# Gated linear attention with a SiLU MLP: q scaled by the reciprocal of alpha's reverse product instead of by a second scan

## The chip, the cores and the metric

The kernel runs on one core of one Trainium2 chip. The metric is the device time of one execution in microseconds. Profiles show one execution, taken by the hardware profiler. The engines are named PE (TensorE, the matrix products), DVE (VectorE), ACT (ScalarE), POOL (GpSimd) and SP (SyncE, which issues most transfers).

## The reference

Two blocks follow each other. The first is a recurrent attention over 4 batches of 8 heads, 768 tokens and a head dimension of 48; the second is an MLP with SiLU on the 3072 tokens of 384 features that come out of it.

```python
for t in range(S):
    state = alpha[:, :, t, :, None] * state + np.einsum('bhd,bhe->bhde', k[:, :, t], v[:, :, t])
    y[:, :, t] = np.einsum('bhd,bhde->bhe', q[:, :, t], state)
...
h = x @ w_in
g = h * (1.0 / (1.0 + np.exp(-h)))
return (g @ w_out).astype(np.float32)
```

All of alpha lies between 0.8 and 1. The weights `w_in` (384 x 2048) and `w_out` (2048 x 384) arrive in double precision and are converted on the chip.

## The kernel before, in words

**Chunks.** Each of the 4 sequences of 768 tokens is cut into 6 chunks of 128 tokens: 24 chunks, numbered n = 0 to 23. Within a chunk the recurrence is turned into products. Let u(t) be the product of alpha over the tokens after t up to the chunk's end, and P the product over the whole chunk. Then k(t) u(t) is the key as it counts at the end of the chunk, and q(t) / u(t) is the query that takes this back to its own token. Scores are products of the two, with later tokens masked out; what earlier chunks left in the state `st` counts with the factor P. All of it is per feature, and the tiles hold the 8 heads as 4 pairs, with the features on the partitions and 4 segments of 129 places along the row: one separating place and 128 tokens. A row so has 4 x 129 = 516 places.

**What VectorE does for a chunk** (function `products`, lines 766 to 793, and `quotient`, lines 795 to 812):

- L775: a scan over the row from right to left multiplies alpha up into `u`. The constant tile `one` starts each segment anew.
- L778: the first place of each segment, the product P over the chunk, goes to `least`, held above 2^-64.
- L786, or L790 and L792: `kp` = k times `u`.
- L803: the reciprocal of the four values of `least`, put at the segment starts of the tile `inv`, which holds zeros elsewhere.
- L805: a second scan, from left to right, multiplies alpha up onto 1/P. It gives `p` = (alpha(1) ... alpha(t)) / P, which is 1/u(t).
- L812: `p` = q times `p`, the scaled query.

Both scans read the tile `al` of alpha, which ScalarE copies out of PSUM (L764) for the first chunks, and VectorE transposes into place (L739) for the later ones.

**Two stages.** For n below 8 (`NA`), `products` calls `quotient` directly, and both follow the order in which they are written, as do the instructions marked `settled`. From n = 8 on, the work of a step is spread over four slots: scores of the chunk before, `products`, `quotient`, and then values, states and `flip`. There the VectorE instructions are placed by a scheduler, which interleaves them with other work, while TensorE's products keep the order in which they are written.

**Other work on the same engines.** The MLP runs beside the attention in pieces that `fill` hands out by due times: products with `w_in` into three PSUM banks `ps_m` (first `enter_plain`, later `enter`, which combines blocks so as to need fewer products, with sums `xc` and `wx` of blocks made ahead of them), the SiLU on ScalarE, sums on VectorE (L1018, L1106, L1123), and products with `w_out` into `ps_o` (`leave`). VectorE also converts the weights in the first 110 us (L675 to L678) and, later, reduces alpha and the weights to their extremes (L728), by which a flag is set at the end. Attention ends at about 435 us; the rest is MLP.

**Buffers.** `u` has one buffer (`upool`), `kp` two in the first stage and one later, `p` two.

Of the kernel before, what the change touches and what calls it, by code (L numbers as in the profile page):

```python
# [8 lines left out]
F32 = mybir.dt.float32  # L9
# [5 lines left out]
ALU = mybir.AluOpType  # L15
# [341 lines left out]
def quotients(  # L357
# [20 lines left out]
    dve, act, gps = nc.vector, nc.scalar, nc.gpsimd  # L378
# [9 lines left out]
    def settled(ins):  # L388

        return tc.keep_in_program_order(ins) if stated[0] else ins  # L390
# [13 lines left out]
    NP = H // 2  # L404
# [6 lines left out]
    W = C + 1  # L411
# [7 lines left out]
    def pool(name, bufs=1, space=None):  # L419
        kw = {} if space is None else {"space": space}  # L420
        return ctx.enter_context(tc.tile_pool(name=name, bufs=bufs, **kw))
# [3 lines left out]
    fix = pool("fix")  # L425
# [20 lines left out]
    def ps_attn(n=C):  # L446
        return ps_a.tile([128, 512], F32, name="ps_a").rearrange("p (j c) -> p j c", c=n)
# [37 lines left out]
    def load(n, names="akq"):  # L485
        if n == NT:
            return
        c = ctxs.setdefault(n, dict(zip(("ci", "b"), divmod(n, B))))
        b, rows = c["b"], slice(c["ci"] * C, c["ci"] * C + C)
        for name, src in (("a", alpha), ("k", k), ("q", q)):  # L490
            if name not in names:
                continue
            x = src[b, :, rows, :]
            if n < NA:
                c[name] = nat[name][n % NIN]
                settled(nc.sync.dma_start(c[name][:, :, 0:D], x.transpose([1, 0, 2])))
                continue

            c[name] = late["quads"][name]
            for u in range(2):
                for i in range(2):
                    r = 64 * u + 32 * i
                    nc.sync.dma_start(
                        c[name][r : r + 32, 32 * (1 - i) :][:, 0 : 4 * NP * D].rearrange(
                            "p (g c) -> p g c", g=NP),
                        x[u::2].rearrange("h (b j) d -> b h (j d)", j=4))
# [40 lines left out]


    seg = [(fix if i == 0 else spare).tile([128, NP * W + 1], F32, name=f"al{i}") for i in range(2)]
    inv = fix.tile([128, NP * W + 1], F32, name="inv")

    kps = [(spare if i else fix).tile([128, NP, C], F32, name=f"kp{i}") for i in range(2)]
    qps = [(spare if i else fix).tile([128, NP * W + 1], F32, name=f"p{i}") for i in range(2)]
# [1 line left out]
    def turns(x, n):  # L557

        return x[(n + 1) % 2]
# [2 lines left out]
    gps.memset(seg[0], 0.0)  # L562
    gps.memset(one, 0.0)
    gps.memset(one[:, 0 : NP * W + 1 : W], 1.0)
    for t in [inv] + seg[1:]:
        gps.memset(t, 0.0)


# [11 lines left out]
    least = fix.tile([128, NT, NP], F32, name="least")  # L580
# [152 lines left out]
    def tokens(t):  # L733

        return t[:, 1 : NP * W + 1].rearrange("p (j c) -> p j c", c=W)[:, :, 0:C]

    def turned(x, to):
        x = x[:, 32:].rearrange("p (g j d) -> p g j d", j=4, d=D)
        dve.transpose(to.rearrange("p g (b j) -> p g j b", j=4), x[:, :, :, 0:32])  # L739

    def bring(n, names="akq"):

        c = ctxs[n]
        sg = seg[0 if late else n % 2]
        ps = c.setdefault("ps", {})

        for name in names:
            if n >= NA:
                if name == "a":
                    turned(c[name], tokens(sg))  # L750
                    load(n + 1, "a")
                continue
            if n <= GB and name != "a" or n == 6 and name == "q":

                at = "kq".index(name)
                ps[name] = (bank(at) if n == 1 else out_bank(at, 512)).rearrange("p (j c) -> p j c", c=C)
            else:
                ps[name] = ps_attn()
            if n == 0 and name != "a" or n == 1 and name != "q":
                idle(2)  # L760
            for j in range(NP):
                pe.transpose(ps[name][:, j, :], c[name][:, 2 * j : 2 * j + 2, :], ident)
            if name == "a":
                settled(act.copy(tokens(sg), ps[name]))  # L764

    def products(n):

        if "ps" not in ctxs[n]:
            bring(n)
        c = ctxs[n]  # L770
        sg = seg[0 if late else n % 2]
        ps = c.pop("ps")
        end = NP * W
        u = upool.tile([128, end + 1], F32, name="u")
        settled(dve.tensor_tensor_scan(u[:, end - 1 :: -1], sg[:, end:0:-1], one[:, end:0:-1],  # L775
                                       0.0, ALU.mult, ALU.add))

        settled(dve.tensor_single_scalar(least[:, n, :], u[:, 0:end:W], 2.0**-64, ALU.max))  # L778
        kp = c["kp"] = turns(kps, n) if n < NA else kps[0]
        ut = tokens(u)  # L780
        if n >= NA:
            ps["k"] = late["turn"].tile([128, NP, C], F32, name="turn")
            turned(c["k"], ps["k"])
            load(n + 1, "k")
        if n < NA:
            settled(dve.tensor_tensor(kp, ps["k"], ut, ALU.mult))  # L786
            quotient(n, sg, ps["q"])
            return
        j = NP // 2
        dve.tensor_tensor(kp[:, 0:j], ps["k"][:, 0:j], ut[:, 0:j], ALU.mult)  # L790
        k, ut = [x[:, j:].rearrange("p j (e c) -> p j e c", e=2) for x in (ps["k"], ut)]
        dve.tensor_tensor(kp[:, j:].rearrange("p j (e c) -> p j e c", e=2)[:, :, ::-1], k, ut, ALU.mult)  # L792
        c["sg"] = sg

    def quotient(n, sg=None, q=None):

        c = ctxs[n]
        if sg is None:
            if n < NA:
                return  # L800
            sg = c.pop("sg")
        end, iv = NP * W, inv
        settled(dve.reciprocal(iv[:, 0:end:W], least[:, n, :]))  # L803
        p = turns(qps if n < NA else [qps[0], late["p"]], n)
        settled(dve.tensor_tensor_scan(  # L805
            p[:, 0:end], sg[:, 0:end], iv[:, 0:end], 0.0, ALU.mult, ALU.add))
        qp = c["qp"] = tokens(p)
        if q is None:
            q = late["turn"].tile([128, NP, C], F32, name="turn")
            turned(c["q"], q)  # L810
            load(n + 1, "q")
        settled(dve.tensor_tensor(qp, q, qp, ALU.mult))  # L812
# [475 lines left out]
    def start():  # L1288

        nonlocal bridged  # L1290
        w = lambda upto: convert(0, upto)
        products(0)
        products(1)
        load(NIN)
        next(conv[0])
# [19 lines left out]
        bring(2, "kq")  # L1315
        w(6)
        products(2)
        go_on()
        w(7)
# [37 lines left out]
    for step in range(5, STEPS):  # L1357
        stages = [[(scores, 1)], [(products, 0)], [(values, 1)], [(states, 1)]]
        if step < NA:
            stages = stages[0:2] + [stages[2] + stages[3], []]  # L1360
        elif step >= NA:
            stages = [[(land, 1), (scores, 1)], [(products, 0)], [(quotient, 0)],
                      [(values, 1), (states, 1), (flip, 0)]]
        for slot, group in enumerate(stages):
            for stage, lag in group:
                n = step - lag
                if not 0 <= n < NT:
                    continue
                stage(n)
                if stage is values:  # L1370
                    bridged = n + 1
                if stage is states and n + 1 + NIN < NA:
                    load(n + 1 + NIN)
                if stage is states and n + NV < NT:
                    load_v(n + NV)
            if step * SLOTS + slot == (NA + 1) * SLOTS - 1:
                x = decayed.rearrange("p (o i c) -> p o i c", o=2, c=C)
                for r, o in later:
                    gps.memset(x[r, o, :, 0:CH], 0.0)
            fill(step, slot)  # L1380
            if step * SLOTS + slot >= NA * SLOTS - 1 and conv_done[1] == NFT and not late:
                settle()
# [17 lines left out]
    ps = ps_attn()[0:1, 0, 0:1]  # L1400
# [14 lines left out]
@with_exitstack  # L1415
def kernel(
    ctx: ExitStack,
    tc: tile.TileContext,
    q: bass.AP,
    k: bass.AP,  # L1420
    v: bass.AP,
    alpha: bass.AP,
    moe_w_in: bass.AP,
    moe_w_out: bass.AP,
    out: bass.AP,
):


    flag = ctx.enter_context(tc.tile_pool(name="flag", bufs=1))
    small = flag.tile([1, 1], I32, name="small")  # L1430
    args = (q, k, v, alpha, moe_w_in, moe_w_out, out)
    within = quotients(tc, small, *args)
    with tc.If(within < 1, label="general"):
        general(tc, *args)
# [30 lines left out]
```

## Time and profile before

| | us |
|---|---|
| median of 3 runs (548.94 to 550.0) | 549.54 |
| the profiled execution | 549.8 |
| its span, first to last instruction | 548.1 |
| granted TensorE clock, share of full | 0.999 |

The span is divided among engines by busy time, and a chain of work is followed back from the last instruction; both are shown in the prediction. Rows of grouped instructions read: line, engine, operation, output and inputs by name, shapes (partitions x elements), count | busy us, mean ns of one | idle time of the engine just before them and what ended it. A row of a stretch gives start and end, length, and for PE, PEld (weight loads), DVE, ACT and POOL the busy time with the number of instructions, then clock, DMA share and GB/s.

### The profile page before, as it was taken

The page shows a single profiled execution, that of the slowest core. Times are in us where ns is not written, and L with a number is a line of the kernel's source. Part 1 is how long each engine was busy: PE and PEld are TensorE (multiplying, and loading weights), DVE is VectorE, ACT ScalarE, POOL GpSimd, SP SyncE. Part 2 cuts the span into 40 slices and gives each one's busy share as a digit, 9 for nine tenths or more (in the row PEclk, how much of TensorE's full clock was granted, in tenths as well). Part 3 has the DMA queues.
Part 4 walks back from the last instruction along what each step waited for, and adds up shares of the span by engine and source line. Part 5 has one row for each costly group of instructions (what it writes and reads, how often), then busy time and mean ns, then how long its engine had stood idle before and what let it go on. Part 6 is the DMA issues. An engine that isn't in the chain of part 4 may idle for free.

```text
span 548.1 us, 12704 instructions
## 1 busy us (share of the span) xinstructions
PE 538.7 (98%) x5069; PEld 493.1 (90%) x5069; DVE 432.8 (79%) x753; ACT 216.3 (39%) x490; POOL 79.4 (14%) x146
## 2 busy tenths in 40 slices
PE   8899999999999999999999999999999999999996
PEld 8788888998999899899999999998998999999996
DVE  5999789986979799996998986998884796944421
ACT  3655554223333334444444354253264342432200
POOL 4111001131212201111121021021121000001000
PEclk9999999999999999999999999999999999999999
DMA  9999861355445434445455653716742144500001
GB/s 213 301 203 248 220 188 33 94 147 139 111 120 134 122 84 119 122 138 159 123 132 146 186 134 98 212 28 167 192 126 85 54 129 148 166 9 19 12 22 35
DMA packets 99219, 70.12 MB, mean 128 GB/s; under 512 B 56272, under 2 KB 88656, under 8 KB 99152
## 3 DMA queue, kind: packets, MB, share of 16 engines
q1 hardware_dynamic: 97232, 65.30, 46.0%
q0 software_dynamic: 1920, 3.93, 2.1%
q8 instruction: 41, 0.67, 0.5%
q14 instruction: 26, 0.21, 0.1%
HBM read 61.34 MB, written 7.86 MB: 126 GB/s over the span
## 4 chain that ended last, share of the span: by engine, by line
PE 96%; DVE 1%; issue 1%; POOL 0%; ACT 0%; DVEq 0%; ACTq 0%; POOLq 0%
PE ps_m L395 45%; PE ps_o L395 38%; PE ps_a L395 12%; PE ps_a L399 2%; DVE p L805 0%; DVE u L775 0%; PE ps_o L399 0%; POOL g L860 0%; DVE p L812 0%; DVE kp L786 0%; ACT xt L923 0%; ACT g L859 0%; ACT al L764 0%; DVE least L778 0%; ACT o L1130 0%
## 5 line engine op out<-in xcount | busy, mean ns | idle before, releaser
L395 PE MATMUL ps_o<-w_out,g 128*128 128x192 f32 x720 | 125.6, 328 | 0.0
L395 PEld LDWEIGHTS ps_o<-w_out,g 128*128 128x128 f32 x720 | 117.8, 190 | 2.7 <-issue 0.4
L395 PE MATMUL ps_m<-xt,w_in 128*128 128x256 f32 x480 | 111.6, 381 | 0.5 <-ACT xt L923 0.5
L395 PEld LDWEIGHTS ps_m<-xt,w_in 128*128 128x128 f32 x480 | 89.9, 190 | 12.7 <-ACT xt L923 0.8
L395 PE MATMUL ps_o<-wt,g 128*128 128x192 f32 x528 | 91.4, 326 | 0.0
L395 PEld LDWEIGHTS ps_o<-wt,g 128*128 128x128 f32 x528 | 87.3, 190 | 1.7 <-DVE o L1132 0.3
L395 PE MATMUL ps_m<-xc,w_in 128*128 128x256 f32 x288 | 70.6, 381 | 0.0
L1123 DVE TENSOR_TENSOR g<-g 128x512 f32<-128x512 f32 x72 | 49.6, 702 | 14.6 <-PE ps_o L395 12.2
L872 POOL TENSOR_SCALAR_AFFINE_SELECT g<-g 64x256 f32<-64x256 f32 x64 | 36.0, 563 | 165.3 <-ACT g L865 162.1
L395 PEld LDWEIGHTS ps_m<-xc,w_in 128*128 128x128 f32 x288 | 53.7, 190 | 6.7
L1015 ACT ACTIVATE g<-g 128x1024 f32<-128x1024 f32 x32 | 33.2, 1057 | 55.5 <-DVE g L1018 55.5
L1010 ACT COPY g<-ps_m 128x512 f32<-128x512 f32 x64 | 37.0, 587 | 36.7 <-PE ps_m L395 36.6
L395 PE MATMUL ps_m<-xc,wx 128*128 128x256 f32 x192 | 50.1, 383 | 0.0
L1135 POOL DMA_DIRECT2D out_dram<-o x40 | 22.1, 552 | 169.9 <-ACT o L1130 74.9
L1018 DVE TENSOR_TENSOR g<-ps_m,g 128x512 f32<-128x512 f32 x56 | 37.5, 684 | 10.9 <-PE ps_m L395 10.5
L395 PEld LDWEIGHTS ps_m<-xc,wx 128*128 128x128 f32 x192 | 35.2, 190 | 4.1 <-issue 0.4
L775 DVE TENSOR_TENSOR_SCAN u<-al,one 128x516 f32<-128x516 f32 x24 | 29.7, 1236 | 7.0 <-ACT al L764 6.6
L983 ACT ACTIVATE g<-ps_m 128x512 f32<-128x512 f32 x32 | 19.0, 597 | 33.2 <-PE ps_m L395 32.9
L805 DVE TENSOR_TENSOR_SCAN p<-al,inv 128x516 f32<-128x516 f32 x24 | 29.8, 1243 | 2.0 <-PE ps_a L395 1.1
L728 DVE TENSOR_REDUCE seen<-bits 128x1 f32<-128x512 int32 (+1 forms) x33 | 26.2, 820 | 6.0 <-DMA bits<-in_moe_w_in_dram 6.0
L1010 ACT COPY part<-ps_m 128x512 f32<-128x512 f32 x32 | 18.9, 590 | 30.4 <-PE ps_m L395 20.4
L1132 DVE TENSOR_TENSOR o<-ps_o,u 128x192 f32<-128x192 f32 x21 | 7.4, 353 | 26.9 <-PE ps_o L395 11.8
(142 smaller groups left out, 681.4 us busy)
## 6 DMA issues: line engine op xcount, KB each, us to landing
bits<-in_moe_w_in_dram SPq DMA_DIRECT2D x24, 512.0 KB, 5.1
bits<-in_moe_w_out_dram SPq DMA_DIRECT2D x16, 384.0 KB, 3.9
at<-in_alpha_dram SPq DMA_DIRECT2D x64, 96.0 KB, 2.6
kt<-in_k_dram SPq DMA_DIRECT2D x64, 96.0 KB, 2.7
qt<-in_q_dram SPq DMA_DIRECT2D x64, 96.0 KB, 2.8
bits<-in_alpha_dram SPq DMA_DIRECT2D x9, 512.0 KB, 4.0
out_dram<-o POOLq DMA_DIRECT2D x40, 96.0 KB, 2.2
flips<-turn SPq DMA_DIRECT2D x12, 256.0 KB, 2.4
```

What stands on the lines that cost most here:

```text
L395: in_order(nc.tensor.matmul(*args, **kw))
L399: in_order(nc.tensor.transpose(*args))
L728: dve.tensor_reduce(seen[kind][which][:, i : i + 1], x, axis=AX, op=op, apply_absolute_value=True))
L775: settled(dve.tensor_tensor_scan(u[:, end - 1 :: -1], sg[:, end:0:-1], one[:, end:0:-1], 0.0, ALU.mult, ALU.add))
L805: settled(dve.tensor_tensor_scan(p[:, 0:end], sg[:, 0:end], iv[:, 0:end], 0.0, ALU.mult, ALU.add))
L872: gps.affine_select(x, x, pattern=[[0, NP], [1, CH]], compare_op=ALU.is_ge, fill=0.0, base=0, channel_multiplier=-1)
L983: settled(act.activation(gts[grp, h, pair][:, i : i + 2, q % 2, :], ps, AF.Silu))
L1010: act.copy(to, ps)
L1015: return act.activation(x, x, AF.Silu)
L1018: dve.tensor_tensor(to, a, b, op)
L1123: dve.tensor_tensor(cells(grp, h, pair, *to), cells(grp, h, pair, *x), cells(grp, h, pair, *y), ALU.subtract)
L1135: (gps if grp < NG - 1 else nc.sync).dma_start(out[r : r + C, c * HO : (c + 1) * HO], o)
```

## The change

The tile `inv` goes, with its memset on GpSimd. L803 and L805 are replaced by one reciprocal over all 516 places of `u`, written to `p`. `products` hands `u` to `quotient` in place of `sg`, the tile of alpha.

```diff
-    inv = fix.tile([128, NP * W + 1], F32, name="inv")
...
-    for t in [inv] + seg[1:]:
+    for t in seg[1:]:
         gps.memset(t, 0.0)
...
-            quotient(n, sg, ps["q"])
+            quotient(n, u, ps["q"])
...
-        c["sg"] = sg
+        c["u"] = u
...
-            sg = c.pop("sg")
-        end, iv = NP * W, inv
-        settled(dve.reciprocal(iv[:, 0:end:W], least[:, n, :]))
+            u = c.pop("u")
+        end = NP * W
         p = turns(qps if n < NA else [qps[0], late["p"]], n)
-        settled(dve.tensor_tensor_scan(
-            p[:, 0:end], sg[:, 0:end], iv[:, 0:end], 0.0, ALU.mult, ALU.add))
+        settled(dve.reciprocal(p[:, 0:end], u[:, 0:end]))
```

Lines behind the change have numbers three lower in the changed kernel, so that L812 becomes L809. In the listings of the program's order a scan appears as SCALAR_TENSOR_TENSOR, and numbers behind a name tell buffers apart. On VectorE, the first chunk at the start of the program, before:

```order
L775 SCALAR_TENSOR_TENSOR u<-al_161,one 128x516
L778 TENSOR_SCALAR least<-u 128x4
L786 TENSOR_TENSOR kp_165<-ps_o,u 128x512
L803 RECIPROCAL inv<-least 128x4
L805 SCALAR_TENSOR_TENSOR p_167<-al_161,inv 128x516
L812 TENSOR_TENSOR p_167<-ps_o,p_167 128x4x128
```

and in the changed kernel:

```order
L774 SCALAR_TENSOR_TENSOR u<-al_161,one 128x516
L777 TENSOR_SCALAR least<-u 128x4
L785 TENSOR_TENSOR kp_164<-ps_o,u 128x512
L803 RECIPROCAL p_166<-u 128x516
L809 TENSOR_TENSOR p_166<-ps_o,p_166 128x4x128
```

Two rows became one at the same place, and the reciprocal now reads `u`. The second place is VectorE's order at about 273 us of the trace, where the sums `xc` of the MLP's inputs are made between the steps of a chunk. Before:

```order
L601 TENSOR_TENSOR xc<-xt 128x256
L778 TENSOR_SCALAR least<-u 128x4
L1123 TENSOR_TENSOR g<-g 128x2x2x128
L601 TENSOR_TENSOR xc<-xt,xc 128x256
L803 RECIPROCAL inv<-least 128x4
L606 SCALAR_TENSOR_TENSOR xc<-xt,xc 128x256
L1123 TENSOR_TENSOR g<-g 128x2x2x128
L603 TENSOR_TENSOR xc<-xt,xc 128x256
L805 SCALAR_TENSOR_TENSOR p_166<-al_161,inv 128x516
L601 TENSOR_TENSOR xc<-xt,xc 128x256
```

and in the changed kernel:

```order
L600 TENSOR_TENSOR xc<-xt 128x256
L777 TENSOR_SCALAR least<-u 128x4
L803 RECIPROCAL p_165<-u 128x516
L600 TENSOR_TENSOR xc<-xt,xc 128x256
L1120 TENSOR_TENSOR g<-g 128x2x2x128
L605 SCALAR_TENSOR_TENSOR xc<-xt,xc 128x256
L1120 TENSOR_TENSOR g<-g 128x2x2x128
L602 TENSOR_TENSOR xc<-xt,xc 128x256
L727 TENSOR_REDUCE seen_2639<-bits 128x1
L600 TENSOR_TENSOR xc<-xt,xc 128x256
```

The long instruction of the chunk stood after four sums `xc` and stands after one; a reduction L727 has come in between the later sums. TensorE's order is the same in both kernels.

More of the change, by code (lines that the diff above doesn't have):

```diff
@@ L792, in products, with quotient @@
         dve.tensor_tensor(kp[:, j:].rearrange("p j (e c) -> p j e c", e=2)[:, :, ::-1], k, ut, ALU.mult)
-        c["sg"] = sg
-    def quotient(n, sg=None, q=None):
+        c["u"] = u
+    def quotient(n, u=None, q=None):
         c = ctxs[n]
-        if sg is None:
+        if u is None:
             if n < NA:
                 return
-            sg = c.pop("sg")
-        end, iv = NP * W, inv
-        settled(dve.reciprocal(iv[:, 0:end:W], least[:, n, :]))
+            u = c.pop("u")
+        end = NP * W
         p = turns(qps if n < NA else [qps[0], late["p"]], n)
-        settled(dve.tensor_tensor_scan(
-            p[:, 0:end], sg[:, 0:end], iv[:, 0:end], 0.0, ALU.mult, ALU.add))
+        settled(dve.reciprocal(p[:, 0:end], u[:, 0:end]))
         qp = c["qp"] = tokens(p)
```

## The prediction

> **What bounds the kernel now.** I read the busy times first, then the chain of work that ended last, then the waits, then the busy times by stretch. The first two lines below are from the page, the next two are what the page gives for the chain, the fifth is TensorE's one wait for a scaled q.
>
> ```profile
> span 548.1 us, 12704 instructions
> PE 538.7 (98%) x5069; PEld 493.1 (90%) x5069; DVE 432.8 (79%) x753; ACT 216.3 (39%) x490; POOL 79.4 (14%) x146
> PE 96%; DVE 1%; issue 1%; POOL 0%; ACT 0%; DVEq 0%; ACTq 0%; POOLq 0%
> ...
> PE ps_a L395 <- DVE p L812: 0.4, 1, 0.4
> ```
>
> TensorE is busy for 98% of the span and makes up 96% of the chain. It has 548.1 - 538.7 = 9.4 us of idle time in all, so no saving on VectorE can bring more than that, and most of it lies at the two ends, as the stretches show (length, then busy time of PE, PEld, DVE, ACT and POOL):
>
> ```profile
> 0.00:20.00 20.00, 16.77 (x220) 15.24 (x221) 13.72 (x24) 9.63 (x18) 8.28 (x25) 1.00 1.10 230
> 20.00:50.00 30.00, 29.27 (x302) 25.20 (x302) 27.47 (x46) 15.79 (x32) 3.64 (x4) 1.00 1.02 258
> 50.00:110.00 60.00, 59.74 (x590) 52.63 (x589) 52.31 (x99) 28.47 (x63) 6.43 (x10) 1.00 0.54 138
> 110.00:190.00 80.00, 79.74 (x942) 72.49 (x942) 65.84 (x116) 25.75 (x78) 17.68 (x30) 1.00 0.50 132
> 190.00:310.00 120.00, 120.00 (x1205) 110.13 (x1207) 111.86 (x189) 51.96 (x121) 19.57 (x35) 1.00 0.49 133
> 310.00:420.00 110.00, 110.00 (x1084) 100.23 (x1077) 91.03 (x152) 48.80 (x118) 16.49 (x30) 1.00 0.50 131
> 420.00:548.10 128.10, 123.23 (x740) 117.23 (x739) 70.58 (x133) 35.85 (x66) 7.32 (x15) 1.00 0.23 67
> ```
>
> From 20 to 420 us TensorE lacks only 0.73 + 0.26 + 0.26 = 1.25 us. VectorE is nearly as full there: idle for 2.5, 7.7, 14.2, 8.1 and 19.0 us in the five stretches, 51.5 of 400 us. It is the second bound, close behind the first, and the change puts its work there. Only the opening is carried by VectorE; the chain in that window, in order of time:
>
> ```profile
> 6.06 1.25 DVE u L775
> ...
> 8.09 0.10 DVE inv L803
> 8.18 0.02 issue
> 8.21 1.25 DVE p L805
> ...
> 9.54 0.69 DVE p L812
> 10.24 1.15 DVE u L775
> ...
> 12.29 1.25 DVE p L805
> ...
> 13.63 0.70 DVE p L812
> ...
> 14.47 1.61 PE ps_a L395 x25
> ```
>
> Here both edited instructions stand on the path, once for each of the first two chunks. Everywhere else they lie beside TensorE.
>
> **The change part by part.** For each of the 24 chunks it removes a reciprocal of four elements and a scan of 516, and adds a reciprocal of 516. The rows by shape (busy us, mean ns of one):
>
> ```profile
> L805 DVE TENSOR_TENSOR_SCAN p<-al,inv 128x516 f32<-128x516 f32 x24 | 29.8, 1243 | 2.0 <-PE ps_a L395 1.1
> L803 DVE RECIPROCAL inv<-least 128x4 f32<-128x4 f32 x24 | 4.2, 175 | 0.4
> L728 DVE TENSOR_REDUCE seen<-bits 128x1 f32<-128x512 int32 x24 | 15.4, 674 | 6.0 <-DMA bits<-in_moe_w_in_dram 6.0
> L728 DVE TENSOR_REDUCE seen<-bits 128x1 f32<-128x1024 f32 x9 | 10.9, 1209 | 0.0
> L728 DVE TENSOR_REDUCE seen<-at 128x1 f32<-128x384 int32 x12 | 6.0, 543 | 0.0
> L812 DVE TENSOR_TENSOR p<-turn,p 128x512 f32<-128x512 f32 x16 | 11.0, 688 | 0.3
> ```
>
> *Removed*: 1.243 + 0.175 = 1.42 us a chunk. *Added*: the whole-tile reciprocal occurs nowhere in this trace, so its price must be bounded. The small one is the only row of that operation. The reductions, which also have one input, give the fixed part: between 512 and 1024 elements (1209 - 674) / 512 = 1.045 ns an element, which leaves 1209 - 1024 x 1.045 = 139 ns fixed; between 384 and 1024 it is 1.041 ns and 143 ns. I take 142 ns. The small reciprocal's 175 ns then leave 33 ns for four elements, 8.25 ns each, and 516 elements take 142 + 516 x 8.25 = 4.4 us. With the other fixed part, 139 ns, it is 9 ns and 4.8 us: the upper end.
>
> The lower end comes from other neighbours. An operation on as many elements, the maximum that writes `least`, takes nearly as long as the small reciprocal (shortest, median, longest):
>
> ```profile
> L778 DVE TENSOR_SCALAR least<-u x24: 161/170/598, 7.3 to 396.6; 128x4 f32<-128x4 f32 x24
> L803 DVE RECIPROCAL inv<-least x24: 164/174/181, 8.0 to 396.8; 128x4 f32<-128x4 f32 x24
> ```
>
> By the medians the reciprocal needs only 4 ns more for its four elements, 1 ns each on top of about 1.04: 142 + 516 x 2.04 = 1.2 us. And if it ran like the multiplication of L812, it would be 0.69 us. So the price lies between 0.69 and 4.8 us. I choose 4.4 us: the maximum also takes a bound as a second operand and reads every 129th element, so its fixed part need not be the reciprocal's, and the plain one-input rows, on which the fixed part can be separated from the slope, are the nearest relatives.
>
> [...]
>
> *The sum.* At 4.4 us each chunk gives VectorE 4.4 - 1.42 = 3.0 us more. In the opening nothing covers it: two chunks, 2 x 3.0 = **6.0 us** on the path. The other 22 fall, by the starts of the small reciprocals, 3, 3, 5, 6 and 5 into the five stretches:
>
> ```profile
> 20.00:50.00 30.00, 0.51 (x3) 1.00 1.02 258
> 50.00:110.00 60.00, 0.51 (x3) 1.00 0.54 138
> 110.00:190.00 80.00, 0.89 (x5) 1.00 0.50 132
> 190.00:310.00 120.00, 1.06 (x6) 1.00 0.49 133
> 310.00:420.00 110.00, 0.88 (x5) 1.00 0.50 131
> ```
>
> That is 9, 9, 15, 18 and 15 us of new work against idle time of 2.5, 7.7, 14.2, 8.1 and 19.0. What hides the edit is this idle time and nothing else: VectorE sits there waiting for a TensorE product or a ScalarE copy, and a late VectorE finds it ready. Not all of it serves: idle time ahead of a chunk's reciprocal is gone before the lateness arises, and a late sum can make TensorE wait at once, which makes VectorE's next input late too. Two waits show the kind:
>
> ```profile
> DVE g L1123 <- PE ps_o L395: 12.2, 8, 3.5
> ...
> DVE g L1018 <- PE ps_m L395: 10.5, 8, 3.0
> ```
>
> In the fourth stretch VectorE is 93% busy with no idle TensorE beside it, so most idle time can be used. I take three quarters: 1.9, 5.8, 10.6, 6.1 and 14.2 us are covered, and 7.1 + 3.2 + 4.4 + 11.9 + 0.8 = **27.4 us** are not. Sum: +33.4 us. The profiled execution took 549.8 us (its span and 1.7 us around it), which is 0.3 us above the median of 549.54: 549.8 + 33.4 = 583.2, less 0.3, is 583. With all idle time used it is 6.5 + 1.3 + 0.8 + 9.9 + 0 = 18.5, and 574; with half, 40.2, and 596. At 4.8 us and half it would be 604, at 4.3 us and all of it 572.
>
> *Moved.* TensorE's order is unchanged, so whatever VectorE delays, TensorE cannot go round. On VectorE the reciprocal stands where the scan stood or a few rows earlier. It matters at the sums `xc` at 273 us (second order listing above), which TensorE's products `ps_m<-xc` take as they come: before, the long instruction stood after four of them, now after one. This is why I don't let the fourth stretch absorb more. ScalarE's conversions and one weight load move by a place or two. No new wait between engines arises: the reciprocal reads `u` from VectorE itself, and the next scan that overwrites the single `u` buffer stands behind it on the same engine.
>
> *Smaller parts*: one memset less on GpSimd in the first 4 us, where VectorE waits for ScalarE's copy of alpha and not for GpSimd: nothing. The accuracy bound `least` is still computed.
>
> **The rivals.** *A quick reciprocal* (0.69 to 1.2 us) ends on the other side. Its place is the opening, its price up to 0.73 us a chunk, and it decides as soon as an element costs less than the scan's (1243 - 142) / 516 = 2.1 ns. The first chunk's gain is cut short, because the second scan of alpha waits for its copy:
>
> ```profile
> 9.24 0.59 ACT L764 COPY al<-ps_a 128x512 f32<-128x512 f32 x1 [3.29 <-PE ps_a L399]
> ```
>
> The copy ends at 9.83 and the scan starts at 10.15 now, so 0.3 us there and 0.73 us in the second chunk: 1.0 us. Afterwards TensorE has 1.25 us to give and waits for a scaled q for 0.4. So 548.5 us at best and 549.5 at 1.2 us. For it speak the medians of L778 and L803; against it the 33 ns above the one-input rows. [...]
>
> *A middling reciprocal* of 3 to 6 ns an element. At 5 ns it takes 2.7 us, 1.3 us more a chunk: 2.6 us in the opening; the stretches get 3.9, 3.9, 6.5, 7.8 and 6.5 us, of which three quarters of the idle time leave 2.0 + 0 + 0 + 1.7 + 0. Sum 6.3, 556 us. The two ways of reading the small reciprocal lie on both sides of it, which speaks for it; no row gives it.
>
> *TensorE's clock falls during the new waits.* At the start four transposes take 1.08 us and later 0.60, by the rows
>
> ```profile
> 4.18 1.08 PE L399 MATMUL ps_a<-ident,an 128*128 128x128 f32 x4
> ...
> 8.55 0.60 PE L399 MATMUL ps_a<-ident,an 128*128 128x128 f32 x4
> ```
>
> so a TensorE that has not been busy for long is slower. If ten of the new waits were long enough to bring this back for 2 us each, that is about 10 us more, 593. It is held within the forecast.
>
> **How the numbers follow.** Slow reciprocal (7 to 9 ns an element): 0.60, with a time of 583 us. Middling: 0.17, 551 to 570. Quick: 0.23, 548.4 to 549.6, about half of it below the 0.2% (1.1 us) that a measurement of this kernel can tell from no change. So faster 0.11, same 0.14 (with the lowest of the middling ones), slower 0.75. The range runs from 549, which takes in the middling cases and about a third of the quick ones, to 600, beyond half of the idle time; the slow case alone is 571 to 600.
>
> **What would show it right or wrong.** The group of the new line must show a mean near 4.4 us; below 2 us the forecast is wrong at its first step. VectorE's busy time must rise by 72 us to about 505. The second score product must start near 20.5 us in place of 14.47. In the stretch that held 190 to 310 VectorE must come close to full, and TensorE must wait for VectorE in `ps_m` and `ps_a`, by some 27 us between the opening and the last attention chunk, and the tail behind it must keep its 128 us. If the reciprocal has its price and TensorE waits far less, the share of idle time that I let cover it was too small.

## The result, and the profile after

The changed kernel takes 568.52 us (568.13 to 568.6, 4 runs) beside 549.39 us for the kernel before (548.94 to 550.0, 4 runs): a ratio of 1.0346 with a 95% interval of 1.0328 to 1.0364, **19.1 us slower**. Slower was forecast, with 583 us and a range from 549 to 600.

The page of the changed kernel: span, busy times, the engines' shares of the chain that ended last, and the group of the new line.

```profile
span 566.8 us, 12677 instructions
PE 544.3 (96%) x5069; PEld 494.3 (87%) x5069; DVE 474.1 (84%) x729; ACT 215.6 (38%) x490; POOL 72.6 (13%) x145
...
PE 63%; DVE 28%; DMA 3%; issue 2%; ACT 2%; SPq 0%; DVEq 0%; POOL 0%; ACTq 0%; POOLq 0%
...
L803 DVE RECIPROCAL p<-u 128x516 f32<-128x516 f32 x24 | 80.9, 3371 | 0.1
```

The chain, which ran through TensorE for 96% before, now runs through VectorE for 28%. The new reciprocal takes 3.37 us, not 4.4, so a chunk gives VectorE 3.37 - 1.42 = 1.95 us more, and the 24 chunks 80.9 - 29.8 - 4.2 = 46.9 us. VectorE's busy time rose by 41.3 us, somewhat less than that; some of its other instructions took a little less time than before (the 72 sums `g` at L1123, for one, 48.5 us after 49.6).

To see where the time went, the start of the same matrix product (of 5069 in the same order) is compared in two traces, with the first product of each set equal. The difference is TensorE's lag. The next rows are the stretches of the changed kernel, cut near the places where the stretches of before end when shifted by the lag (columns as in the prediction):

```profile
0.00:20.00 20.00, 16.15 (x111) 14.32 (x115) 14.03 (x18) 5.67 (x10) 5.55 (x22) 0.83 1.06 214
20.00:56.20 36.20, 32.66 (x419) 27.20 (x411) 34.01 (x47) 19.08 (x38) 5.67 (x6) 1.00 0.89 224
56.20:121.20 65.00, 60.75 (x591) 52.75 (x591) 59.66 (x96) 29.10 (x65) 6.88 (x10) 1.00 0.53 129
121.20:202.80 81.60, 80.29 (x943) 72.49 (x942) 73.96 (x112) 25.70 (x78) 15.44 (x30) 1.00 0.48 127
202.80:327.20 124.40, 121.10 (x1205) 109.94 (x1207) 121.94 (x182) 51.71 (x121) 17.21 (x35) 1.00 0.48 128
327.20:438.90 111.70, 110.10 (x1083) 100.27 (x1076) 99.87 (x147) 48.53 (x118) 14.48 (x30) 1.00 0.49 129
438.90:566.80 127.90, 123.27 (x741) 117.34 (x739) 70.58 (x133) 35.80 (x66) 7.33 (x15) 0.99 0.22 67
```

Against the lengths of before (30, 60, 80, 120, 110 and 128.1 us) the stretches grew by 6.2 (with the opening in it), 5.0, 1.6, 4.4, 1.7 and -0.2 us: 18.7, the difference of the spans. The tail without attention kept its length. VectorE still has 29.5 us of idle time in the five stretches between opening and tail, while TensorE, which lacked 1.25 us there before, now lacks 14.0.

### The profile page after: what moved, and what is told of

Its sections match the earlier page's. It is cut to its first block, busy times and chain, and to the rows that moved or that the text cites. A ratio compares the mean times of both kernels' runs of the same rounds, so it can differ in the third digit from the quotient of the medians.

```text
span 566.8 us, 12677 instructions
## 1 busy us (share of the span) xinstructions
PE 544.3 (96%) x5069; PEld 494.3 (87%) x5069; DVE 474.1 (84%) x729; ACT 215.6 (38%) x490; POOL 72.6 (13%) x145
## 4 chain that ended last, share of the span: by engine, by line
PE 63%; DVE 28%; DMA 3%; issue 2%; ACT 2%; SPq 0%; DVEq 0%; POOL 0%; ACTq 0%; POOLq 0%
PE ps_o L395 29%; PE ps_m L395 28%; DVE p L803 7%; PE ps_a L395 7%; DVE u L774 2%; DVE w_in L676 2%; DVE w_in L677 2%; DVE g L1015 2%; DMA bits<-in_moe_w_out_dram 1%; DVE g L1120 1%; DVE g L1103 1%; DVE p L809 1%; DVE w_out L676 1%; DVE w_in L674 1%; DVE xc L600 1%
## 5 line engine op out<-in xcount | busy, mean ns | idle before, releaser
L803 DVE RECIPROCAL p<-u 128x516 f32<-128x516 f32 x24 | 80.9, 3371 | 0.1
L1120 DVE TENSOR_TENSOR g<-g 128x512 f32<-128x512 f32 x72 | 48.5, 687 | 14.2 <-PE ps_o L395 11.9
L869 POOL TENSOR_SCALAR_AFFINE_SELECT g<-g 64x256 f32<-64x256 f32 x64 | 29.9, 467 | 169.0 <-ACT g L862 155.3
L395 PEld LDWEIGHTS ps_a<-p,kp 48*64 48x64 f32 (+1 forms) x640 | 20.6, 147 | 10.7 <-issue 6.6
L395 PE MATMUL ps_a<-p,kp 48*64 48x64 f32 (+2 forms) x640 | 24.6, 260 | 3.8 <-DVE p L809 3.8
```

What stands on the lines that cost most here:

```text
L395: in_order(nc.tensor.matmul(*args, **kw))
L803: settled(dve.reciprocal(p[:, 0:end], u[:, 0:end]))
L869: gps.affine_select(x, x, pattern=[[0, NP], [1, CH]], compare_op=ALU.is_ge, fill=0.0, base=0, channel_multiplier=-1)
L1120: dve.tensor_tensor(cells(grp, h, pair, *to), cells(grp, h, pair, *x), cells(grp, h, pair, *y), ALU.subtract)
```

## The experiments

All times are medians; the difference is to the kernel before on the same chip. The lag is TensorE's behind the trace of before, at the places where that trace stands at 21, 50, 110, 190, 310 and 420 us:

```
kernel                              us      diff     21    50   110   190   310   420
changed                           568.52   +19.1    2.9   6.4  11.2  12.8  17.2  19.0
quick operation                   547.53    -2.1   -1.1  -1.6  -1.8  -1.8  -2.0  -2.2
reciprocal for n < 2              552.77    +3.3    2.2   2.8   3.2   3.2   3.1   3.1
reciprocal for n < 8              561.11   +11.5    2.0   6.9  11.1  11.1  11.1  11.0
reciprocal for n >= 8             557.11    +7.5   -0.3  -0.4  -0.2   1.1   5.6   7.4
two halves                        567.20   +17.6    5.0   8.0  12.6  12.6  17.1  17.9
before + 130 places               557.89    +8.3    2.1   3.4   5.8   6.5   8.4   8.4
before + 290 places               569.91   +20.3    3.0   6.7  10.8  12.7  17.4  19.9
changed + 141 places              577.68   +28.2    3.4   9.6  15.9  17.7  24.5  28.3
changed + 290 places              592.94   +43.4    5.4  14.5  23.9  27.1  39.1  43.5
changed, 4 rounding buffers       569.79   +20.2    2.3   6.4  10.6  12.2  16.6  20.3
before, 4 rounding buffers        549.34    -0.2    0.0  -0.3  -0.3  -0.3  -0.3  -0.2
changed, 4 rounding, 6 weights    567.75   +18.2    5.1   7.6  10.7  12.3  16.7  18.7
```

### A quick operation in the reciprocal's place

```diff
-        settled(dve.reciprocal(p[:, 0:end], u[:, 0:end]))
+        settled(dve.tensor_tensor(p[:, 0:end], u[:, 0:end], one[:, 0:end], ALU.add))
```

> The changed kernel with the whole-tile reciprocal replaced by one addition of the same shape (u + one, 516 places), so q is not divided by u. Theory 1 (the price of the reciprocal is the cause: 3.37 us against 1.42 us removed, 1.95 us more on VectorE per chunk): with an operation of about 0.69 us everything is given back, 548.4 to 549.6 us, since TensorE has only 1.25 us idle between 20 and 420 us and about 1 us to gain in the opening. Rival A (the scheduler's new order of VectorE's instructions is the cause): the time stays above 558 us. Rival B (a shorter operation pays beyond the opening too): below 546 us.

Measured: 547.53 us, ratio 0.9968 (0.9956 to 0.9979); the operation takes 0.69 us. The whole loss goes with the long instruction, though the rest of the change and most of VectorE's new order stay: rival A falls. The gain of 2.1 us is more than theory 1 allowed (548.4 at the least), but it arises where it was expected: 1.6 us of it by 50 us, and hardly anything later, so rival B falls too. This also says what there is to win: a reciprocal that cost no more than an addition would be worth 0.3%.

### The price: two halves, and two other sizes

```diff
-        settled(dve.reciprocal(p[:, 0:end], u[:, 0:end]))
+        mid = end // 2
+        settled(dve.reciprocal(p[:, 0:mid], u[:, 0:mid]))
+        settled(dve.reciprocal(p[:, mid:end], u[:, mid:end]))
```

> The changed kernel with the reciprocal cut into two of 258 places. If its price is a fixed part of about 142 ns and 6.26 ns an element ((3371 - 142) / 516), each half takes 142 + 258 x 6.26 = 1.76 us and the time is 568 to 571 us. If a large part of the 3.37 us were fixed (a start-up of the divide), each half would take over 2.2 us and the time would rise above 575 us.

Measured: 567.20 us (2 runs, 566.38 to 568.01), just under the band, which two runs 1.6 us apart can't tell from it. The groups of the two halves, and of the extra reciprocals of 130 and 290 places in the runs below:

```profile
L804 DVE RECIPROCAL p<-u 128x258 f32<-128x258 f32 x24 | 42.2, 1759 | 0.0
...
L805 DVE RECIPROCAL p<-u 128x258 f32<-128x258 f32 x24 | 41.6, 1732 | 0.0
```

```profile
L808 DVE RECIPROCAL more<-p 128x130 f32<-128x130 f32 x24 | 23.1, 963 | 0.6
```

```profile
L808 DVE RECIPROCAL more<-p 128x290 f32<-128x290 f32 x24 | 47.1, 1963 | 0.6
```

From 130 to 290 places it is (1963 - 963) / 160 = 6.25 ns a place, from 290 to 516 (3371 - 1963) / 226 = 6.23. With 6.25 the fixed part is 963 - 812 = 151 ns, and four places take 176 ns: the small reciprocal's 175. From 4 to 516 places the price is linear, and no part of it beyond 0.15 us is a start-up.

### Early and late chunks apart

```diff
+        if n < NA:
+            settled(dve.reciprocal(p[:, 0:end], u[:, 0:end]))
+        else:
             settled(dve.tensor_tensor_scan(
                 p[:, 0:end], sg[:, 0:end], iv[:, 0:end], 0.0, ALU.mult, ALU.add))
```

with the small reciprocal kept for the scan, and likewise with the condition turned round, or `n < 2`.

> The whole-tile reciprocal for chunks 0 to 7 alone, the small reciprocal and the scan for chunks 8 to 23. Theory 1, with TensorE's lag read off the two traces (12.7 us behind at the end of the first stage, 18.95 at the end): 560 to 563 us. Rival, the prediction's own shares (6 us opening, 10 to 12 us in the two early stretches at 3.0 us a chunk; at the measured 1.95 us a chunk 3.9 + 4.0 + 0.05): 556 to 558 us.

> The small reciprocal and the scan for chunks 0 to 7, the whole-tile reciprocal for chunks 8 to 23. Theory 1 by the lag of the traces: 6.2 us of the loss arises there, 555 to 556 us. Rival (the late stretches lose little of their own, the late steps of the lag are an echo of the lateness from the first stage): 549 to 552 us. Rival (the prediction's shares at the measured price, three quarters of the idle time used): 549.4 + 5.6, 555 us; so the run tells the echo apart, not the shares.

> The whole-tile reciprocal for the first two chunks alone, the small reciprocal and the scan for the other 22. In the changed kernel TensorE is 4.2 us behind at the second score product and 2.9 us at 23 us. If the opening's loss is kept to the end: 549.5 + 2.9 = 552.4 us (552 to 553). If nothing were won back after the second score product: 553.7 us. If VectorE's idle time behind it (7.7 us between 50 and 110 us) swallows it: 549.5 to 550.5 us.

Measured: 561.11 (1.0196 to 1.0228), 557.11 (1.012 to 1.0151) and 552.77 us (1.0047 to 1.0075). The two parts add up: 11.5 + 7.5 = 19.0. The late chunks lose 7.5 us of their own, a little over the expected 6.2, so the late steps of the lag are no echo of the early ones. The first two chunks cost 3.3 us, and nothing behind them swallows it.

### The same VectorE time without the change, and other doses

```diff
         settled(dve.tensor_tensor_scan(
             p[:, 0:end], sg[:, 0:end], iv[:, 0:end], 0.0, ALU.mult, ALU.add))
+        settled(dve.reciprocal(more[:, 0:290], p[:, 0:290]))
```

A dose is the VectorE time that a kernel adds to each chunk. The half dose has 130 places here. The two larger doses add the same kind of instruction (141 or 290 places of `u`) to the changed kernel.

> The kernel before, with its scan and small reciprocal, plus one reciprocal of 290 places per chunk behind the scan, whose result nobody reads: 142 + 290 x 6.26 = 1.96 us more VectorE time a chunk, as the change adds (1.95 us), and nothing else of the change. Theory 1 (time on VectorE is the cause, whatever it computes): 565 to 570 us. Rival A (where the scheduler puts the long instruction matters as well; here it leaves the place before the sum that TensorE waits for at 385 us of the changed kernel's trace, which cost 1.8 us there): 563 to 567 us, and no step of the lag at that place.

> As the run with 290 places, with 130 places: 142 + 130 x 6.26 = 0.96 us more VectorE time a chunk, half the dose. Theory 1 with cover that is used up place by place (opening 2 x 0.96 = 1.9 us; beyond it idle time of 2.5, 7.7, 7.0, 7.2, 0.5, 4.9, 2.7, 7.3, 4.9 and 6.8 us in stretches that get 2.9, 2.9, 2.9, 1.9, 1.9, 1.9, 1.9, 1.9, 1.9 and 1.0 us): 549.5 + 1.9 + 0.4 + 1.4 = 553, at most 557 us. If the loss were proportional to the added time, half of 19: 559 us.

> The changed kernel plus one reciprocal of 141 places per chunk whose result nobody reads, 142 + 141 x 6.26 = 1.02 us: with the change itself 2.97 us more VectorE time a chunk, the dose that the prediction reckoned with. If its sum was right but for the price (three quarters of the idle time cover), 583 us. If the loss grows as from half to full dose (8.3 us at 0.96, 19.0 at 1.95, so 10.8 us for each further microsecond), 580 us. If all idle time covers, 574 to 576 us.

> The changed kernel plus one reciprocal of 290 places per chunk whose result nobody reads: 1.95 + 1.96 = 3.9 us more VectorE time a chunk, double dose, 94 us in all. Straight on from the smaller doses: 590 us. If VectorE's idle time (51.5 us of 400) runs out, nearly every added microsecond counts: three quarters covered gives 605 us. VectorE's busy time must then be over 97% of the stretch up to the last attention chunk.

Measured: 569.91 us for the same time in the order of before (1.0352 to 1.0395; 568.18 to 571.13 in 4 runs). Whether its result is used does not matter here (569.91 beside 568.52 us); its time does. Rival A had its place right: the step of 1.8 us at 385 us of the changed kernel's trace, all that its fifth stretch lost, is absent from this run's lag. But another 2.5 us come up between 310 and 420 us instead, so the total is not below the changed kernel's.

The doses of 0.96, 1.95, 2.97 and 3.91 us a chunk cost 8.3, 19.1, 28.2 and 43.4 us: of the time added over 24 chunks (23, 47, 71 and 94 us) 36, 41, 40 and 46%. The opening, where 3.3 of 3.9 us reached the end, is in this; without the lag at 21 us and the first two chunks the shares are 29, 38, 38 and 44%. Even the half dose, 23 us against 51.5 us of idle VectorE, costs over a third of itself. My 553 to 557 us for it was too low, because I used up the idle time first. The dose of 2.97 us met none of its three forecasts: 577.68 us lies between full cover (576 at most) and the straight line (580), and three quarters of cover (583) was too dear. The double dose came within 3 us of the straight line (590), far from the 605 of three quarters. At the double dose VectorE is busy for 429.26 of 440 us, 97.6% (third busy time):

```profile
20.00:460.00 440.00, 410.88 (x4200) 366.33 (x4200) 429.26 (x604) 173.01 (x410) 59.41 (x108) 0.98 0.49 130
```

VectorE is then nearly full itself; a larger dose was not run. TensorE's granted clock, the third figure from the end, is 0.98 in this row; at 2.97 us a chunk it was 0.99 between 20 and 446 us, and in the changed kernel and at the half dose 1.00. By estimate that is up to 440 x 0.02 = 8.8 and 426 x 0.01 = 4.3 us of the losses of 43.4 and 28.2; if all of it reached the end, the waits alone would be 37 and 34% of the added time. The two were not separated.

### Is ScalarE's queue the way in which VectorE delays TensorE early on?

Between 50 and 110 us VectorE had 7.7 us of idle time for 5.9 us of new work, and TensorE still lost 5 us. The largest step of the changed kernel's lag behind the opening, 1.9 us, comes at 70 us. TensorE's row and ScalarE's rows there, from the timeline:

```profile
70.50 0.66 PE L399 MATMUL ps_a<-ident,an 128*128 128x128 f32 x4 [1.84 <-ACT g L856]
```

```profile
67.83 0.56 ACT L658 ACTIVATE up<-bits 128x384 int32<-128x384 uint32 x1 [0.99 <-DVE w_out L677]
68.29 0.58 ACT L980 ACTIVATE g<-ps_m 128x512 f32<-128x512 f32 x1
69.42 0.56 ACT L658 ACTIVATE up<-bits 128x384 int32<-128x384 uint32 x1 [0.55 <-DVE w_out L677]
69.87 1.06 ACT L856 COPY g<-ps_a 128x512 f32<-128x512 f32 x2
```

TensorE waits for a PSUM bank that ScalarE's copy of the scores (L856) frees; the copy stands behind a rounding (L658), and the rounding waits for VectorE, which frees its buffer (L677). More buffers take this wait away:

```diff
-    raw = first.enter_context(tc.tile_pool(name="raw", bufs=4))
-    upp = first.enter_context(tc.tile_pool(name="upp", bufs=2))
+    raw = first.enter_context(tc.tile_pool(name="raw", bufs=6))
+    upp = first.enter_context(tc.tile_pool(name="upp", bufs=4))
```

The first pair of runs changes `upp` alone, in the changed kernel and in the one before; the third changes both in the changed kernel and starts two transfers more at the beginning.

> The changed kernel with four buffers in place of two for ScalarE's rounding results (up, L658), so that ScalarE's copies of the scores no longer stand behind a rounding that waits for VectorE. Theory 2 (between 50 and 110 us VectorE has idle time enough, but its lateness reaches TensorE through ScalarE's queue: rounding waits for VectorE, the copy of the scores stands behind it, TensorE waits for the copy's PSUM bank): 2 to 4 us are given back, 564.5 to 566.5 us. Rival (VectorE itself is late there, ScalarE only shows it): 568 us, as the changed kernel.

> The kernel before with four buffers in place of two for ScalarE's rounding results; VectorE's and TensorE's order is unchanged. TensorE lacks 0.26 us between 50 and 110 us there, so both theories expect 549 to 549.7 us, no difference; it is the control for the run with four buffers in the changed kernel.

> The changed kernel with four buffers for ScalarE's rounding results and six in place of four for the raw weights. With four rounding buffers alone ScalarE's wait only moved from VectorE's sum to the weights' transfer, whose buffer VectorE frees. Theory 2 (TensorE's wait at 70 us of the changed kernel's trace comes through ScalarE's queue and the weights' buffers): with two pieces more in flight the step of 1.9 us there goes, and that of 1.0 us at 90 us, so 565.5 to 567 us. Rival (VectorE's own work sets the pace between 50 and 110 us): the lag at 110 us is again 10 to 11 us and the time 568 to 570 us.

Measured: 569.79 us (1.0352 to 1.038), 549.34 (0.9987 to 1.0005) and 567.75 us (1.0314 to 1.0342), the last between the two bands of its forecast. With four rounding buffers the rounding waits for the transfer of the weights instead, into buffers that VectorE frees:

```profile
65.28 0.56 ACT L658 ACTIVATE up<-bits 128x384 int32<-128x384 uint32 x1 [2.85 <-DMA bits<-in_moe_w_out_dram]
```

With six weight buffers too, TensorE's waits for the copy at 70 and 90 us, 1.84 and 0.83 us in the changed kernel, are gone, as theory 2 wanted. But the lag at 110 us is 10.7 as against 11.2, since a wait came up behind them. The row of the changed kernel, and that of this run:

```profile
112.39 0.55 PE L395 MATMUL ps_a<-vn,kn 128*32 128x48 f32 x32 [0.74 <-DVE kp L785]
```

```profile
111.92 0.55 PE L395 MATMUL ps_a<-vn,kn 128*32 128x48 f32 x32 [2.35 <-DVE kp L787]
```

The lag at 21 us was 2.2 us larger in this run, so TensorE's lag alone doesn't settle it. VectorE's own does. The same product `kp`, that of the last chunk of the first stage, in the kernel before, in the changed kernel and in this run:

```profile
100.59 0.69 DVE L786 TENSOR_TENSOR kp<-ps_a,u 128x512 f32<-128x512 f32 x1
```

```profile
111.65 0.69 DVE L785 TENSOR_TENSOR kp<-ps_a,u 128x512 f32<-128x512 f32 x1
```

```profile
111.17 0.69 DVE L787 TENSOR_TENSOR kp<-ps_a,u 128x512 f32<-128x512 f32 x1
```

VectorE is 11.1 us late there, and 10.6 us with the buffers: nearly the same, whichever way TensorE waited before. ScalarE's queue was the messenger; VectorE itself is behind there, and TensorE meets it at the next place where it needs a result, the 2.35 us at `kp`. As the cause of the loss theory 2 falls. VectorE still idles 5.3 us of the 65 in this stretch of the changed kernel; why that idle time can't serve was not settled.

## Why the prediction was right, and where it was off

**The sign and the mechanism: right.** It rested on three things: that VectorE's new time is far above the 1.42 us removed (2.4 times, where 3.1 was forecast), that VectorE is the second bound, and that its idle time covers only a part. All three hold, and the run with an unused instruction of the same length shows that nothing else of the change is needed.

**The size: 14 us too much, and held by a wide range.** At 568.5 us the time lies below the 571 to 600 us of the slow case, on which the forecast stood, and within the 551 to 570 of the middling one, which had a chance of 0.17; the price of an element, 6.25 ns, lies between the two (3 to 6 and 7 to 9). The forecast's own rule for the cover gives 13.5 us at the measured price (worked out below), where 19.1 were measured, so the error of the price made good for an error of the rule, and more than that. That the sum came as near as it did is in part luck.

**The signs named.** The new line's mean is 3.37 us, not near 4.4; VectorE's busy time is 474 us, not 505; the second score product starts at 18.66 us, not at 20.5; TensorE lacks 14.0 us between the opening and the tail, not some 27. Right were the stretch that held 190 to 310 us, where VectorE is busy for 121.94 of 124.40 us, and the tail, which kept its length.

**The price: a mis-sized term.** "33 ns for four elements, 8.25 ns each" took 142 ns as the fixed part, from the reductions. The reciprocal's own is 151 ns, and 6.25 ns an element. The 9 ns of difference, carried from 4 elements to 516, became over 1 us: 4.4 us in place of 3.37. The measured price is a little below the slow case's own 7 to 9 ns. The quick rival's reading, 2 ns from the medians of two operations with equal element counts, was further off. Six times the 1.04 ns that the reductions need for an element is 6.24.

**The opening: two errors, both towards too much.** Forecast were 2 x 3.0 = 6.0 us. At the measured price it is 3.9, and the two chains show it (start, length):

```profile
6.02 1.24 DVE u L774
...
8.05 3.30 DVE p L803
11.44 0.69 DVE p L809
12.13 1.15 DVE u L774
...
14.07 3.29 DVE p L803
17.46 0.69 DVE p L809
```

The second scaled q is ready at 18.15 in place of 14.33, 3.8 us later. TensorE's score product is 4.2 us late, at 18.66 us and not at the 20.5 forecast. Then 1.84 us come back (the lag falls from 4.73 to 2.89 us): before, TensorE waited once more there, and the changed kernel doesn't. The row of before:

```profile
20.45 0.37 PE L395 MATMUL ps_a<-vn,g 128*32 128x48 f32 x14 [1.64 <-issue]
```

I had not looked at which waits of the opening would be swallowed. What is left, 2.9 us here and 3.3 in the run with two chunks, is half the forecast.

**The cover: the wrong rule.** "I take three quarters" gave 7.1, 3.2, 4.4, 11.9 and 0.8 us for the stretches. Measured are some 3.3 (6.2 less the opening's 2.9), 5.0, 1.6, 4.4 and 1.7. With the right price the rule would have given 3.9 + 0.1 + 0 + 5.6 + 0 and 3.9 for the opening, 13.5 us in all: too little. At the dose it reckoned with, 2.97 us a chunk, it gave 33.4 where 28.2 were measured: too much. So the total of 33 was not wrong by the price alone. Idle time in a stretch of 100 us is not a store that is emptied before TensorE notices: already the smallest dose tried, 23 us in all, lost 36% of itself, and the larger ones 40 to 46%. Where a stretch is full on a short scale, the rule is near: between 190 and 230 us of before VectorE was busy for 39.51 of 40 us, and the lag there grows by 3.6 us for two chunks of 1.95. Where it is not full, between 50 and 110 us, the idle time hardly helped: TensorE lost some 5 of the 5.9 us added.

**The place named for the fourth stretch: right, and small.** The prediction pointed at the sums `xc` behind which the reciprocal now stands. The chain of the changed kernel runs through just these to TensorE:

```profile
288.49 3.28 DVE p L803
291.77 0.28 DVE xc L600
...
293.58 0.34 DVE xc L602
293.91 1.13 DVE seen L727
295.04 0.33 DVE xc L600
...
296.37 1.13 PE ps_m L395 x4
```

The reciprocal and the reduction L727 that came in between the sums both lie on it. The step there is 0.7 us. The larger part of that stretch, 3.3 us, comes between 212 and 237 us, where the sum behind a reciprocal frees what ScalarE and then TensorE wait for:

```profile
207.86 3.28 DVE p L803
211.14 0.56 DVE g L1015
...
211.77 0.59 ACT part L1007
...
212.41 2.86 PE ps_m L395 x12
```

**TensorE waits for VectorE in `ps_a` and `ps_m`: right, in part by way of ScalarE.** The longest waits of TensorE:

```profile
PE ps_a L395 <- DVE p L809: 3.8, 3, 1.5
PE ps_a L399 <- ACT g L856: 2.7, 2, 1.8
PE ps_m L395 <- ACT part L1007: 2.4, 2, 1.6
PE ps_o L395 <- DVE o L1129: 1.6, 2, 0.9
```

**The quick rival: its time was close.** It put a quick operation at 548.5 us at best; the run gave 547.5. For the opening 1.0 us was reckoned; the gain was 1.1 us at 21 us and 1.6 by 50 us.

**The clock rival: it happens, once ahead of the kernel's end, and costs little here.** The clock was 0.50 from 12 to 18 us of the changed kernel, which cost some 0.4 us; see the last section. That a TensorE that has not been busy for long is slower, as the rival puts it, was my reading of two rows of one trace (1.08 and 0.60 us); behind a wait of 3.22 us, in the run with 2.97 us a chunk, it was not slower.

## What to carry to other kernels

A row of four elements didn't price an operation of 516 here: 9 ns too little for its fixed part made 4.4 us out of 3.37. Carry the bounds on to the time, or find a second size. An engine that was 87% busy beside a full one was not 13% free: over a third of the added time reached the end, at the smallest dose too (8.3 of 23 us, with the opening), because the full engine met the late one again at other places where it needed a result. And a wait that names another engine, here ScalarE, may only pass on the lateness: the buffers that took that wait away moved it to a later place, and the lag at 110 us was 10.7 us beside 11.2.

## What was not expected of the hardware

TensorE's granted clock fell to half in the opening, once, after a wait of 1.55 us. The stretches of the changed kernel (the third figure from the end is the clock), and TensorE's rows:

```profile
10.00:12.00 2.00, 0.64 (x4) 0.40 (x4) 1.90 (x2) 0.67 (x1) 0.00 (x0) 0.97 1.10 344
12.00:14.00 2.00, 1.81 (x16) 1.78 (x16) 1.97 (x5) 0.00 (x0) 0.00 (x0) 0.50 1.03 390
...
16.00:18.00 2.00, 2.00 (x11) 2.00 (x11) 1.90 (x2) 0.51 (x1) 0.17 (x1) 0.50 1.43 199
18.00:20.00 2.00, 2.00 (x29) 1.66 (x32) 1.82 (x5) 0.14 (x1) 0.00 (x0) 0.82 0.70 78
```

```profile
12.19 2.08 PE L395 MATMUL ps_a<-p,kp 48*128 48x128 f32 x16 [1.55 <-DVE p L809]
...
15.11 3.62 PE L395 MATMUL ps_m<-ident 128*128 128x128 f32 x16
18.66 1.17 PE L395 MATMUL ps_a<-p,kp 48*128 48x128 f32 x16
```

In the two microseconds that hold most of the wait for the first scaled q TensorE was busy for 0.64; the clock is 0.82 in the row of 18 to 20 us, and 1.00 between 20 and 22. The 16 filler products at 15.11 us took 3.62 us, and 1.95 in the trace of before. As VectorE's second q is ready only at 18.15 us, this cost some 0.4 us. The four runs of the changed kernel had clocks of 0.992, 0.997, 0.996 and 0.992 and took 568.57, 568.13, 568.6 and 568.46 us, so it weighs little in them.

The length of such a wait alone doesn't decide. In the run with six weight buffers the 16 products behind a wait of 1.58 us at the same place took 1.16 us, as in the trace of before, and not 2.08. In the run with 2.97 us a chunk those behind a wait of 3.22 us took 1.16 too, and the clock was 1.00 from 0 to 20 and from 20 to 40 us:

```profile
12.29 1.16 PE L395 MATMUL ps_a<-p,kp 48*128 48x128 f32 x16 [1.58 <-DVE p L811]
```

```profile
19.60 1.16 PE L395 MATMUL ps_a<-p,kp 48*128 48x128 f32 x16 [3.22 <-DVE p L811]
```

What decides is open. In the run with six weight buffers the clock was 0.96 in the first 20 us and 0.75 from 20 to 30 us, and the lag at 21 us is 5.1 in place of 2.9 us. With two halves that lag is 5.0 us; the clock of its profiled execution is 0.992 over the whole span, as in the changed kernel, and where it was lower was not shown. With four rounding buffers the lag grew by 3.7 us between 310 and 420 us, and by 1.8 in the changed kernel; that run was 1.3 us slower than the changed kernel, with a clock of 0.993 over the span. That these differences come from the clock was not shown.
